# A third LayerNorm row buffer in the output stage, gate/up sums made there, and other moves in a two-layer transformer kernel

## The chip, the cores and the metric

The kernel runs on one core of a Trainium2 chip. The metric is the device time of one execution in microseconds (us).

## The reference

Two layers, each an attention block with a linear kernel (block A) and a gated feed-forward block (block B), on a sequence of 2048 rows of 1024 values, in bfloat16:

```python
def reference(A_x, A_wqkv, A_wo, B_x, B_w_gate, B_w_up, B_w_down):
    def _A_ref(x, wqkv, wo):              # 32 heads of 32
        ...                               # q, k, v = x @ wqkv
        phi = lambda t: jnp.where(t > 0, t + 1, jnp.exp(t)) + 1e-6
        pq, pk = phi(q), phi(k)
        kv = jnp.einsum("bhsd,bhse->bhde", pk, v)
        z = jnp.einsum("bhsd->bhd", pk)
        num = jnp.einsum("bhqd,bhde->bhqe", pq, kv)
        den = jnp.einsum("bhqd,bhd->bhq", pq, z)[..., None] + 1e-6
        ...                               # (num / den) @ wo
    def _B_ref(x, w_gate, w_up, w_down):  # 3584 hidden values
        ...                               # ((x @ w_gate) * (x @ w_up)) @ w_down
    x = A_x
    x = x + _A_ref(_layernorm(x, axis=-1), A_wqkv, A_wo)
    x = x + _B_ref(_layernorm(x, axis=-1), B_w_gate, B_w_up, B_w_down)
    x = x + _A_ref(_layernorm(x, axis=-1), A_wqkv, A_wo)
    x = x + _B_ref(_layernorm(x, axis=-1), B_w_gate, B_w_up, B_w_down)
    return x
```

## The kernel before

In each layer the stages are: projections of q and k in "quads" of pairs, a stage that forms the small key/value products ("G stage"), the last held projections, the output stage (the product with `wo`, row tile by row tile), then gate/up and down in two passes of half the sequence. The gate/up and down products are done by a two-level scheme that replaces some matmuls by sums of blocks (Strassen's idea), and VectorE makes those sums.

Three pieces of it carry the argument. The first is the norm of a row of queries. There are two buffers for the finished row (`asb`), but one for the reciprocals (`rden`):

```python
def norm(i):
    ...                                            # VectorE: product, reduction, add
    P.add("dve", lambda e: e.reciprocal(rden, den), ...)
    b = i % 2
    P.add("pool", lambda e: e.tensor_tensor(out=asb[b]..., in1=rden..., op=ALU.mult), ...)
    P.add("sp", lambda e: e.dma_start_transpose(xnT[:, :, i * 128:(i + 1) * 128], asb[b]), ...)
```

The second is the loop of the output stage. `norm`, `pack` (a copy of weights from DRAM to DRAM), `ring_issue` (weight loads) and `step_t` (the transpose of a LayerNorm row) all put their transfers into one queue, that of SyncE (SP):

```python
for i in range(NST):                               # 16 row tiles
    if na[0] < NST:
        if i % 3 == 2:
            norm(tok[na[0]]); na[0] += 1
    elif RG["n"] < NR:
        ring_issue()
    if first and i % 3 == 1:
        pack()
    nxt.step_t(1)                                  # transpose of a LayerNorm row, by DMA
    nxt.b1_one()
    if i >= 2:
        nxt.start(i - 2)                           # statistics of a row, VectorE
    y_grp(tok[i], 0, i)                            # 8 matmuls, then an add on VectorE
    y_seed(i + 1)                                  # ScalarE seeds a bank for the next row
    nxt.b2_one()                                   # ScalarE normalises a row into O_XN[n % 2]
    y_grp(tok[i], 1, i)                            # 8 matmuls, then a copy on ScalarE
    ...
    if nxt.t_next >= 8 and RG["tq"] is None:       # eight rows transposed:
        RG["tq"] = t_ops(0)                        # block sums of the first half, VectorE
    ...
```

The third is the head of a gate/up pass, where the first layer makes the sums for its first two units just before the first matmuls, and the second layer issues the loads of its block sums:

```python
pre = ("P1A", "P1B") + (("D2A", "D2B") if jit else ()) + ("P5A", "P5B")
...
if jit:                                            # first layer, first pass
    prep_s(n0)                                     # four sums on VectorE
    prep_s(n0 + 1)
early = not first
if early:
    for q in "25":
        sums(1, q)                                 # second layer: loads from scratch
for tk in pre:
    emit(0, tk, True)
```

Of the kernel before, what the change touches and what calls it, by code (L numbers as in the profile page):

```python
# [180 lines left out]
def build_kernel(nc, A_x, A_wqkv, A_wo, B_w_gate, B_w_up, B_w_down, out):  # L181
    _, S, D = A_x.shape
# [55 lines left out]
    O_DEN = take(128)  # L238
    O_RDEN = take(128)
    O_RZ = take(64)  # L240
# [66 lines left out]
    KTA = [dkey("ta%d" % i) for i in range(2)]  # L307
    KTL = [dkey("tl%d" % i) for i in range(2)]
    KTF = [dkey("tf%d" % i) for i in range(NST)]
# [12 lines left out]
    with ExitStack() as es:  # L322
# [48 lines left out]
        den = vf(O_DEN, 32)  # L371
        rden = vf(O_RDEN, 32)
        rz = vf(O_RZ, 8)
# [101 lines left out]
        class LN:  # L475
# [12 lines left out]
            def dst(self, n):  # L488
                if self.to == "A0":
                    return xrt[n], r_xr(n)  # L490
                return xn[n % 2], R(O_XN[n % 2], D * 2)

# [42 lines left out]
            def transpose(self, n):  # L535
                d, r = self.dst(n)
                i = self.order[n]
                if self.use_dma:
                    P.add("sp", lambda e: e.dma_start_transpose(xnT[:, :, i * 128:(i + 1) * 128], d),
                          rd=r, wr=r_xT(i * 128, (i + 1) * 128), dma_sem=KTF[i] if self.to == "A0" else KTL[n % 2])  # L540
                    return
# [320 lines left out]
        def layer_A(lnp, nxt, first):  # L862
# [147 lines left out]
            def norm(i):  # L1010
# [7 lines left out]
                      rd=R(O_DEN, 128), wr=R(O_DEN, 128))  # L1018
                P.add("dve", lambda e: e.reciprocal(rden, den), rd=R(O_DEN, 128), wr=R(O_RDEN, 128))  # L1019
                b = i % 2  # L1020
                P.add("pool", lambda e: e.tensor_tensor(out=asb[b].rearrange("p (h c) -> p h c", c=32), in0=pbuf.rearrange("p (h c) -> p h c", c=32),  # L1021
                                                       in1=rden.unsqueeze(2).broadcast_to([128, 32, 32]), op=ALU.mult),
                      rd=R(O_P[i % 2], D * 4) + R(O_RDEN, 128), wr=R(O_A[b], D * 2))
                P.add("sp", lambda e: e.dma_start_transpose(xnT[:, :, i * 128:(i + 1) * 128], asb[b]),
# [70 lines left out]
            for n, (kind, p) in enumerate(items):  # L1095
# [10 lines left out]
                if first:  # L1106
                    i = NPL + len(LNX) + n
                    for j in range(2):
                        if i < NST:
                            job(n, 2 * j, lambda i=i, j=j: lnstep(i, j))  # L1110
                    c, m = 9 - max(NPL - 3, 0), len(items)
                    if (n + 1) * c // m > n * c // m:
                        job(n, 3, pack)
                elif n >= 2:
                    if n == 9:
                        job(n, 0, lambda: rl.update(o=O_XN[0]))
                    job(n, 0, lnp.flush_b)
                    job(n, 2, lnp.flush_a)

# [136 lines left out]
            for i in range(NST):  # L1256
# [9 lines left out]
                nxt.b1_one()  # L1266
                if i >= 2:
                    nxt.start(i - 2)
                y_grp(tok[i], 0, i)
                y_seed(i + 1)  # L1270
                nxt.b2_one()
                y_grp(tok[i], 1, i)
                if not first and i >= 8:
                    stash(i - 8)
# [8 lines left out]
        def layer_B(lnp, nxt, first):  # L1283
# [6 lines left out]
            if not is_last:  # L1290
                nxt.use_dma = True
                nxt.on_act = False

# [195 lines left out]
            def gateup(ps_, ticks, l2):  # L1489
# [16 lines left out]

                pre = ("P1A", "P1B") + (("D2A", "D2B") if jit else ()) + ("P5A", "P5B")
                tpl = tp_ops(ps_, l2)
# [44 lines left out]

                if jit:
                    prep_s(n0)
                    prep_s(n0 + 1)
                early = not first
                if early:
                    for q in "25":
                        sums(1, q)  # L1560
                for tk in pre:
                    emit(0, tk, True)
                for p in range(NP):
                    for tk in order:
                        emit(p, tk)
# [19 lines left out]
            def down(ps_, ticks, tail):  # L1585
# [37 lines left out]
                tr, ha_ = [flat(O_T + 3584 * i) for i in range(3)], [flat(O_HA + 3584 * i) for i in range(4)]  # L1623
                sbuf2 = {"4": [xbuf(i) for i in range(3)], "5": tr if "4" in l2d else [xbuf(i) for i in range(3)], "3": [xbuf(i, 1 - ps_) for i in range(3)]}
                tbuf2 = {"4": [flat(RE), flat(RE + 3584), flat(O_XN[0])], "5": [xbuf(3), ha_[0], ha_[1]], "3": [ha_[2], ha_[3], xbuf(3, 1 - ps_)]}
                r4 = [(vf(o, 512), R(o, 2048)) for o in (RC, RC + 2048, RB + 28672, RB + 30720)]
# [184 lines left out]
            def dticks0(q, t):  # L1811
# [5 lines left out]
                if q == "3" and t < 2:  # L1817
                    tq.pop(0)()
                    tq.pop(0)()
                if q == "5" and t == 3 and not is_last:  # L1820
                    for k in range(4):
# [8 lines left out]
            def dticks1(q, t):  # L1830
# [11 lines left out]
                if q == "7" and t == 3:  # L1842
                    for c in (2, 4):
                        tw_load("q", c)
                if q == "5" and t == 3:
                    for w in "kq":
# [5 lines left out]
                if q == "3":  # L1852
                    s_make(nxt.order, 0)[t]()
                    stash(12 + t)
# [18 lines left out]
            lnp.use_dma = False  # L1873
            lnp.on_act = False
        dh0 = D // 2
        dma(x_res[:, 0, 0:dh0], x2[0:128, 0:dh0], r_x(0, 0, dh0), KX[0])
# [62 lines left out]
```

## Time and profile before

| | kernel before |
|---|---|
| median time | 1449.56 us (3 runs, 1448.41 to 1450.8) |
| span of the profiled execution | 1449.1 us (run of 1450.86 us) |
| TensorE busy | 1426.2 us, 98% |
| VectorE / ScalarE / GpSimd busy | 84% / 46% / 10% |
| idle time of TensorE in its waits view | 19.4 us |

TensorE is the bound, and the only thing to win is its idle time. The prediction shows where that lies. Two lines more are from the waits views of ScalarE and VectorE of the kernel before; after the colon stand the sum in us, the number of times, and the longest.

```profile
ACT arena L468 <- DMA arena<-arena: 16.3, 7, 4.2
DVE arena L765 <- DMA arena<-arena: 7.1, 2, 4.6
```

L468 is the normalisation of a row on ScalarE, L765 a block sum on VectorE. Both wait for a DMA inside the on-chip memory, that is, for a transpose.

### The profile page before, as it was taken

How to read it: one execution, taken by the hardware profiler on the slowest of the kernel's cores; microseconds unless marked ns; L12 is line 12 of the kernel's file. 1: busy time of each engine (PE TensorE's matmuls, PEld its weight loads, DVE VectorE, ACT ScalarE, POOL GpSimd, SP SyncE). 2: the span in 40 equal slices, each digit the busy share in tenths (PEclk: the TensorE clock that was granted, in tenths of full speed). 3: DMA queues.
4: the chain of work that ended last, by engine and by line, in shares of the span. 5: the costliest groups of instructions: out<-in, count | busy, mean ns of one | idle time of the engine just before them, and what ended most of it. 6: DMA issues, size and time to landing. Idle time of an engine off the chain costs nothing.

```text
span 1449.1 us, 21876 instructions
## 1 busy us (share of the span) xinstructions
PE 1426.2 (98%) x8186; PEld 787.3 (54%) x8186; DVE 1218.2 (84%) x2376; ACT 665.6 (46%) x1378; POOL 147.2 (10%) x176
## 2 busy tenths in 40 slices
PE   8999998999999999999999999999999999999999
PEld 3444443455545666664554444446666475666547
DVE  6987887999978799988779878778888887888888
ACT  5673245444420266661037823467776004777400
POOL 2212521000010000002010046210000100000000
PEclk9999999999999999999999999999999999999999
DMA  8578977997786777777985166667775866777653
GB/s 261 88 203 225 198 171 155 289 328 266 266 252 215 235 248 260 245 256 264 268 262 145 40 175 151 184 166 263 261 260 191 277 237 231 265 259 257 207 195 119
DMA packets 270459, 320.22 MB, mean 221 GB/s; under 512 B 161936, under 2 KB 212880, under 8 KB 270352
## 3 DMA queue, kind: packets, MB, share of 16 engines
q1 hardware_dynamic: 270352, 318.82, 72.3%
q8 instruction: 64, 1.05, 0.3%
q14 instruction: 43, 0.35, 0.1%
HBM read 236.45 MB, written 73.40 MB: 214 GB/s over the span
## 4 chain that ended last, share of the span: by engine, by line
PE 80%; DVE 11%; DMA 4%; issue 2%; ACT 2%; POOL 1%; SPq 1%; POOLq 0%; DVEq 0%; ACTq 0%
PE ps L1319 27%; PE ps L1400 16%; PE ps L1736 14%; PE ps L919 6%; PE ps L1138 6%; PE ps L1654 5%; DVE arena L765 3%; PE ps L890 3%; DMA arena<-arena 3%; PE ps L1240 2%; DVE arena L451 2%; DVE arena L768 1%; DVE arena L1015 1%; DVE arena L1012 1%; DVE arena L612 1%
## 5 line engine op out<-in xcount | busy, mean ns | idle before, releaser
L765 DVE TENSOR_TENSOR arena<-arena 128x512 f16<-128x512 f16 (+8 forms) x1015 | 497.8, 518 | 61.6 <-ACT arena L1404 33.6
L1319 PE MATMUL ps<-arena 128*128 128x512 f16 x1888 | 457.3, 379 | 2.7 <-ACT ps L1348 2.0
L768 DVE SCALAR_TENSOR_TENSOR arena<-ps,arena 128x512 f16<-128x512 f32 (+3 forms) x545 | 353.6, 664 | 68.7 <-PE ps L1736 26.9
L1400 PE MATMUL ps<-arena 128*128 128x256 f16 x2184 | 287.5, 273 | 2.2 <-DMA arena<-sp_scratch 1.3
L1319 PEld LDWEIGHTS ps<-arena 128*128 128x128 f16 (+1 forms) x1888 | 182.8, 98 | 165.6 <-ACT ps L1348 6.3
L1400 PEld LDWEIGHTS ps<-arena 128*128 128x128 f16 (+1 forms) x2184 | 212.1, 98 | 93.1 <-ACT arena L1404 6.9
L1736 PE MATMUL ps<-arena 128*128 128x512 bf16 (+1 forms) x1120 | 244.7, 379 | 0.0
L1736 PEld LDWEIGHTS ps<-arena 128*128 128x128 f16 x1120 | 109.6, 98 | 130.2
L1324 ACT ACTIVATE arena<-ps 128x512 f32<-128x512 f32 x224 | 133.7, 597 | 82.2 <-PE ps L1319 64.3
L1404 ACT ACTIVATE arena<-ps 128x256 f32<-128x256 f32 x351 | 125.1, 385 | 26.9 <-PE ps L1400 22.0
L919 PE MATMUL ps<-arena 128*128 128x512 f16 (+1 forms) x560 | 123.2, 379 | 2.7 <-ACT arena L926 0.9
L1138 PE MATMUL ps<-arena 128*128 128x512 bf16 x512 | 116.1, 379 | 0.0
L1240 PE MATMUL ps<-arena 128*128 128x512 bf16 x512 | 111.5, 379 | 3.6 <-ACT ps L1234 3.3
L454 POOL TENSOR_SCALAR arena<-arena 128x1 f32<-128x1 f32 x64 | 24.5, 383 | 804.5 <-DVE arena L453 804.5
L1410 ACT COPY ps<-ps 128x256 f32<-128x256 f32 x182 | 66.4, 365 | 75.0 <-DVE arena L768 29.4
L451 DVE BATCH_NORM_STATS2 arena<-arena 128x6 f32<-128x512 bf16 x128 | 88.2, 689 | 13.9 <-DMA arena<-in_A_x_dram 6.6
L1021 POOL TENSOR_TENSOR arena<-arena 128x1024 f16<-128x1024 f32 x32 | 76.4, 2389 | 184.3 <-DVE arena L1019 167.1
L1348 ACT COPY ps<-ps 128x512 f32<-128x512 f32 x112 | 65.4, 584 | 61.4 <-PE ps L1319 50.2
L1682 ACT COPY arena<-ps 128x256 f32<-128x256 f32 x8 | 3.0, 372 | 197.1 <-PE ps L1654 197.1
L919 PEld LDWEIGHTS ps<-arena 128*128 128x128 f16 x560 | 54.0, 98 | 70.9 <-ACT arena L926 5.1
L890 PE MATMUL ps<-arena 128*128 128x512 bf16 x384 | 85.5, 379 | 3.6 <-ACT arena L555 1.6
L1654 PE MATMUL ps<-arena 128*128 128x256 f16 (+1 forms) x784 | 86.8, 273 | 0.5 <-DVE arena L768 0.3
(61 smaller groups left out, 969.8 us busy)
## 6 DMA issues: line engine op xcount, KB each, us to landing
arena<-w_scratch SPq DMA_DIRECT2D x84, 896.0 KB, 4.6
arena<-t_scratch SPq DMA_DIRECT2D x32, 896.0 KB, 5.8
arena<-in_B_w_down_dram SPq DMA_DIRECT2D x24, 896.0 KB, 5.0
arena<-sp_scratch SPq DMA_DIRECT2D x26, 768.0 KB, 4.2
w_scratch<-arena SPq DMA_DIRECT2D x28, 512.0 KB, 6.3
arena<-w_scratch SPq DMA_DIRECT2D x28, 384.0 KB, 5.2
x_scratch<-arena SPq DMA_DIRECT2D x40, 256.0 KB, 7.4
arena<-x_scratch SPq DMA_DIRECT2D x40, 256.0 KB, 5.9
```

Of the source, the lines that this page charges most:

```text
L765: P.add("dve", lambda e: e.tensor_tensor(out=out, in0=a, in1=b, op=op), rd=rd, wr=wr, prd=prd)
L768: P.add("dve", lambda e: e.scalar_tensor_tensor(out=out, in0=a, scalar=sc, in1=b, op0=ALU.mult, op1=op1), rd=rd, wr=wr, prd=prd)
L890: return [e.matmul(psb(bank), xnT[:, k, i * 128:(i + 1) * 128], t[:, k, h * 512:(h + 1) * 512], start=(k == 0), stop=(k == KT - 1)) for k ...
L919: P.add("pe", lambda e: [e.matmul(psb(bank), a[0][:, k, :], b[0][:, k, :], start=(q in (1, 5) and k == 0), stop=(k == 3), skip_group_check ...
L1138: return [e.matmul(psb(bank), xrt[t][:, jj * 128:(jj + 1) * 128], pk[:, h, t, :], start=(t == tok[0]), stop=(t == tok[NST - 1])) for t in ts]
L1240: return [e.matmul(psb(bank), xnT[:, g, i * 128:(i + 1) * 128], wp[:, g, dh * 512:(dh + 1) * 512], start=(dh == 0 and g == 0), stop=(g == ...
L1319: P.add("pe", lambda e: [e.matmul(psb(bank), w[:, k, :], x[:, k, :], start=(start and k == 0), stop=(k == 3), skip_group_check=True) for k ...
L1324: P.add("act", lambda e: e.activation(t, psb(bank), AF.Copy, scale=SG), prd=[bank], wr=r)
L1400: P.add("pe", lambda e: [e.matmul(psb(bank)[:, 256 * half:256 * half + 256], w[:, k, :], xx[:, k, :], start=(start and k == 0), stop=(k == ...
L1404: P.add("act", lambda e: e.activation(d, src, AF.Copy, scale=sc), prd=[xk], wr=rd_)
L1654: P.add("pe", lambda e: [e.matmul(psb(bank)[:, 256 * half:256 * half + 256], a[:, k, 128 * r:128 * r + 128], b[:, k, :], start=(start and ...
L1736: P.add("pe", lambda e: [e.matmul(psb(bank), hv[:, 7 * hf + k, t * 128:(t + 1) * 128], w[:, k, :], start=(q in "15" and hf == 0 and k == 0 ...
```

## The change

The intent is to close TensorE's gaps by giving the engines that feed it more room. It has five parts: (1) two reciprocal buffers; (2) a third row buffer for LayerNorm rows in the output stage; (3) the first gate/up sums made in the last two rows of the output stage, with the statistics of one row and a normalisation moved behind the first matmuls of gate/up; (4) in the layer change, statistics started in every second quad only, ScalarE normalising under down, and block sums of the next layer made under the fifth product rather than the third; (5) one block-sum load issued under down. The diff, cut to its core:

```diff
-    O_RDEN = take(128)
+    O_RDEN = [take(128) for _ in range(2)]
...
-                return xn[n % 2], R(O_XN[n % 2], D * 2)
+                o = (O_XN + [O_WQ])[n % 3] if self.to == "B" and n < 14 else O_XN[n % 2]
+                return vh(o, D), R(o, D * 2)
...
-                    job(n, 2, lnp.flush_a)
+                    if n % 2:
+                        job(n, 2, lnp.flush_a)
...
-                if i >= 2:
+                if 2 <= i < 15:
                     nxt.start(i - 2)
                 y_grp(tok[i], 0, i)
                 y_seed(i + 1)
-                nxt.b2_one()
+                if i < 15:
+                    nxt.b2_one()
                 y_grp(tok[i], 1, i)
+                if first and i >= 14:
+                    prep_s(i - 14)
...
-                nxt.on_act = False
+                nxt.on_act = True
...
-                pre = ("P1A", "P1B") + (("D2A", "D2B") if jit else ()) + ("P5A", "P5B")
+                pre = ("P1A", "P1B", "P5A", "P5B")
...
-                if jit:
-                    prep_s(n0)
-                    prep_s(n0 + 1)
                 early = not first
                 if early:
-                    for q in "25":
+                    for q in "25"[ps_:]:
                         sums(1, q)
                 for tk in pre:
                     emit(0, tk, True)
+                if ps_ == 0:
+                    lnp.b2_one()
+                    lnp.start(13)
...
+                if q == "4" and t == 0 and not first:
+                    sp_load(1, 1, "2")
...
+                if q == "5":
+                    s_make(nxt.order, 0)[t]()
...
                 if q == "3":
-                    s_make(nxt.order, 0)[t]()
```

Cut are the new semaphores, the use of `rden[i % 2]`, and a shift of scratch buffers for the moved block sums.

More of the change, by code (lines that the diff above doesn't have):

```diff
@@ L307, in build_kernel @@
     KTA = [dkey("ta%d" % i) for i in range(2)]
-    KTL = [dkey("tl%d" % i) for i in range(2)]
+    KTL = [dkey("tl%d" % i) for i in range(3)]
     KTF = [dkey("tf%d" % i) for i in range(NST)]
@@ L371, in build_kernel @@
         den = vf(O_DEN, 32)
-        rden = vf(O_RDEN, 32)
+        rden = [vf(o, 32) for o in O_RDEN]
         rz = vf(O_RZ, 8)
@@ L539, in transpose @@
                     P.add("sp", lambda e: e.dma_start_transpose(xnT[:, :, i * 128:(i + 1) * 128], d),
-                          rd=r, wr=r_xT(i * 128, (i + 1) * 128), dma_sem=KTF[i] if self.to == "A0" else KTL[n % 2])
+                          rd=r, wr=r_xT(i * 128, (i + 1) * 128), dma_sem=KTF[i] if self.to == "A0" else KTL[n % (3 if self.to == "B" and n < 14 else 2)])
                     return
@@ L1018, in norm @@
                       rd=R(O_DEN, 128), wr=R(O_DEN, 128))
-                P.add("dve", lambda e: e.reciprocal(rden, den), rd=R(O_DEN, 128), wr=R(O_RDEN, 128))
+                P.add("dve", lambda e: e.reciprocal(rden[i % 2], den), rd=R(O_DEN, 128), wr=R(O_RDEN[i % 2], 128))
                 b = i % 2
                 P.add("pool", lambda e: e.tensor_tensor(out=asb[b].rearrange("p (h c) -> p h c", c=32), in0=pbuf.rearrange("p (h c) -> p h c", c=32),
-                                                       in1=rden.unsqueeze(2).broadcast_to([128, 32, 32]), op=ALU.mult),
-                      rd=R(O_P[i % 2], D * 4) + R(O_RDEN, 128), wr=R(O_A[b], D * 2))
+                                                       in1=rden[b].unsqueeze(2).broadcast_to([128, 32, 32]), op=ALU.mult),
+                      rd=R(O_P[i % 2], D * 4) + R(O_RDEN[b], 128), wr=R(O_A[b], D * 2))
                 P.add("sp", lambda e: e.dma_start_transpose(xnT[:, :, i * 128:(i + 1) * 128], asb[b]),
@@ L1623, in down @@
                 tr, ha_ = [flat(O_T + 3584 * i) for i in range(3)], [flat(O_HA + 3584 * i) for i in range(4)]
-                sbuf2 = {"4": [xbuf(i) for i in range(3)], "5": tr if "4" in l2d else [xbuf(i) for i in range(3)], "3": [xbuf(i, 1 - ps_) for i in range(3)]}
-                tbuf2 = {"4": [flat(RE), flat(RE + 3584), flat(O_XN[0])], "5": [xbuf(3), ha_[0], ha_[1]], "3": [ha_[2], ha_[3], xbuf(3, 1 - ps_)]}
+                sbuf2 = {"4": [xbuf(i) for i in range(3)], "5": tr if "4" in l2d else [xbuf(1 + i) for i in range(3)], "3": [xbuf(i, 1 - ps_) for i in range(3)]}
+                tbuf2 = {"4": [flat(RE), flat(RE + 3584), flat(O_XN[0])], "5": [xbuf(3) if "4" in l2d else ha_[2], ha_[0], ha_[1]], "3": [ha_[2], ha_[3], xbuf(3, 1 - ps_)]}
                 r4 = [(vf(o, 512), R(o, 2048)) for o in (RC, RC + 2048, RB + 28672, RB + 30720)]
@@ L1874, in layer_B @@
             lnp.on_act = False
+            if not is_last:
+                nxt.on_act = False
         dh0 = D // 2
```

## The prediction

> **What bounds the kernel now.** I read the page's busy shares first, then the times of the slices, then the waits of TensorE, then its timeline gap by gap.
>
> ```profile
> PE 1426.2 (98%) x8186; PEld 787.3 (54%) x8186; DVE 1218.2 (84%) x2376; ACT 665.6 (46%) x1378; POOL 147.2 (10%) x176
> PEclk9999999999999999999999999999999999999999
> ```
>
> TensorE (PE) is busy 98% of the 1449.1 us and its clock is granted in full, so it is the bound almost everywhere, and nothing in the diff takes a matmul away. What can be won is idle time of TensorE. The waits view of TensorE has 19.4 us of it, and the timeline puts it into 23 places. Those that the change can touch:
>
> ```profile
> 180.49 1.04 PE L1191 MATMUL ps<-arena 128*128 128x512 bf16 x4 [1.07 <-DVE arena L1169]
> 185.06 0.39 PE L1191 MATMUL ps<-arena 128*128 128x512 bf16 x1 [1.15 <-DVE arena L1198]
> 225.26 12.26 PE L1240 MATMUL ps<-arena 128*128 128x512 bf16 x56 [1.69 <-ACT ps L1234]
> 237.75 7.08 PE L1240 MATMUL ps<-arena 128*128 128x512 bf16 x32 [0.23 <-DVE arena L1246]
> 248.54 4.49 PE L1319 MATMUL ps<-arena 128*128 128x512 f16 x20 [1.98 <-ACT ps L1348]
> 253.72 6.22 PE L1319 MATMUL ps<-arena 128*128 128x512 f16 x28 [0.69 <-ACT arena L1324]
> 774.72 1.04 PE L919 MATMUL ps<-arena 128*128 128x512 bf16 x4 [0.73 <-DVE arena L939]
> 776.27 6.33 PE L919 MATMUL ps<-arena 128*128 128x512 f16 x28 [0.51 <-ACT arena L926]
> 938.96 21.33 PE L1240 MATMUL ps<-arena 128*128 128x512 bf16 x98 [1.63 <-ACT ps L1234]
> 1212.72 0.60 PE L1400 MATMUL ps<-arena 128*128 128x256 f16 x4 [1.25 <-DMA arena<-sp_scratch]
> ```
>
> Columns: start, length, engine, line, operation, count, and in brackets the idle time before it with what ended it. Two more of the kind, 0.19 and 0.20 us at 782.80 and 789.21, wait for L926. These twelve places hold 11.3 us. The start of the kernel (five gaps, 5.6 us, until 14.65) is untouched, and so are a few small gaps in the gate/up and down stages (2.5 us).
>
> One correction. In steady state eight 512-column matmuls follow each other in 1.73 us (216 ns each), yet one is drawn 379 ns long. The drawn end overlaps the next start by about 0.16 us, so each gap really costs about 0.17 us more than is printed: 11.3 + 12 x 0.17 = 13.3 us. That is the ceiling of this change, 0.9% of the time.
>
> **What the Trainium skill says.** "TensorE: Matmul & The Clock Gate", section "Back-to-back issue gap", gives N/2.4 + 2.5 ns for a matmul by itself, 216 ns at N = 512, and 131 ns for a long stream; the trace's 1.73 us for eight in a stream agrees with the first, not with the second. Over 8186 matmuls this makes an estimated 1419 us of pure issue: the time can't fall far. "Perfetto Trace Analysis", section "Tensor Engine Instruction (MATMUL, LD_WEIGHTS)", says that ScalarE (ACT), VectorE (DVE) and GpSimd (POOL) run their instructions strictly in order; the ACT lines below agree, where one waiting instruction holds up two that TensorE needs. The same page, section "Optimization Strategy", connects gaps with too few buffers and advises making what ends them start sooner, which is the plan of the change. "SBUF — State Buffer", section "SBUF: two separate sides", says that VectorE and GpSimd take a shared port pair as an exclusive lock: VectorE's L1017 takes 181 ns alone and up to 1342 ns beside GpSimd's L1021, so the trace fits. This makes me cautious about the first part below.
>
> **The change part by part.**
>
> *1. Two `rden` buffers.* Before 180.49 the chain is: GpSimd's L1021 waits for a DMA, VectorE's reciprocal L1019 waits for L1021 because there is one `rden`, and L1169, which TensorE needs, stands behind it.
>
> ```profile
> DVE arena L1019 <- POOL arena L1021: 2.8, 1, 2.8
> ```
>
> This wait occurs once. With two buffers L1169 can run when its matmuls end, near 177.9, before TensorE asks for it at 179.3. The two gaps are 2.22 + 0.34 = 2.56 us. But VectorE's next small instruction L612 took 1.68 us beside L1021 instead of 0.28 and may do so again, and then L1198 still comes late for the second gap. I count 1.5 us.
>
> *2. Third row buffer for the LayerNorm rows in the output stage.* ScalarE normalises a row (L468, 1.24 us), a DMA transposes it, and with two buffers row n waits for the transpose of row n-2.
>
> ```profile
> 222.88 1.24 ACT L468 ACTIVATE arena<-arena 128x1024 f16<-128x1024 bf16 x1 [2.99 <-DMA arena<-arena]
> 224.02 0.56 ACT L1248 CAST arena<-ps 128x512 bf16<-128x512 f32 x1
> 224.62 0.59 ACT L1234 CAST ps<-arena 128x512 f32<-128x512 bf16 x1
> ```
>
> The copy L1234 seeds a bank for TensorE and stands behind L468; the 1.69 us gap at 225.26 ends with it. The transpose's median from issue to landing is 3.5 us after about 1.3 us of issue, one row of the loop is 16 matmuls or 3.46 us: with two buffers that is just not enough, with three the row has one loop step more. All L468 waits for DMA sum to 16.3 us in seven places, and most should go. VectorE gains too: its first block sum of the stage waits 4.59 us (until 234.21) for the eighth transpose, which then lets it fall behind at 237.75. Worth: 1.86 + 0.40 in the first layer, 1.80 in the second: 4.1 us, of which I count 4.0. No work is added; the three buffers lie in space that is free then.
>
> *3. First gate/up sums in the output stage, last LayerNorm row after the first matmuls.* At 248.54 TensorE waits for the copies L1348, which stand on ScalarE behind L468 and L1248, themselves behind a late VectorE. VectorE's statistics and final add end at 248.39, then it makes eight sums (3.01 us). After the change these eight are issued in the last two rows, statistics of row 13 (two of 0.69, one of 0.21) and one L468 move behind the first sixteen matmuls, and the D2 products, which need the copies, no longer come ahead of P5. The two gaps are 2.67 + 0.34 = 3.0 us. VectorE's load in the last five rows is then about 3.75 + 3.75 + 4.97 + 4.0 + 2.35 = 18.8 us (from 0.2, 1.6, 0.65, 1.22 and 1.5 us for the five kinds of work in a row) against 17.3 us of TensorE. It ends about 1.5 us late, just in time for P5, but the statistics follow, and the first pair was already tight (VectorE 12.3 of 13 us busy from 249 to 262). I count 2.3 us.
>
> *4. Spread LayerNorms, normalising on ScalarE under down, block sums of pair 0 earlier.* In the second attention layer four statistics come in four successive quads before and in every other quad after. From 753 to 789 VectorE is busy 34.8 of 36 us, and the four gaps there are 1.63 + 0.68 = 2.3 us. Each statistics costs 1.6 us, each normalisation 0.53 us (L471), and about two of the four move out of the full stretch, so the backlog of 1 to 2 us should go. One normalisation that ScalarE inherits lands in a quad where it is already busy about 4.9 of 6 us. Under down ScalarE is nearly free (3.7 of 79 us), and TensorE has no gap there, so moving about ten L471 there (some 5 us of VectorE) gains nothing by itself. I count 1.6 us.
>
> *5. Block sums loaded under down.* The first two-level product of the last gate/up pass waits 1.25 us for its load; issued more than 10 us earlier, it has landed. 1.4 us, counted in full.
>
> Sum: 1.5 + 4.0 + 2.3 + 1.6 + 1.4 = 10.8 us. I take off 1.8 us for new gaps, of which I expect some: statistics inside the first pair, relu buffers that share the LayerNorm row buffer from the tenth quad on, now soon after a later transpose. Predicted: 1449.6 - 9.0 = 1440.6, say 1440.5 us.
>
> **The rivals.** *VectorE takes over as the bound at the seam.* Its work isn't less, only moved; from 235 to 249 it is busy 13.3 of 14 us. Then TensorE meets it a few microseconds later in the first pair, and parts 2 and 3 give 3 us rather than 6.3: 1444. For it speaks the tight first pair; against it the 4.6 us idle before 234.21 and 2.57 us before 224.69, which part 2 frees. *The transposes are held up by the in-order DMA queue, not by buffers.* Around 201 to 210 an L468 row's transpose was issued behind one of L1021's that waited for GpSimd until 209. Then a third buffer only moves the wait: part 2 gives 1 us, total 1443.5. Against it: later in the stage no such transpose is in the way, and the waits go on. *New waits outweigh*: the relu buffer's wait for the transpose costs 2 to 4 us in one quad, ScalarE stalls on L468 while copies queue behind it under down: 1446. *Everything goes and the seams run clean*: 13.3 us, 1436.
>
> **Range and chances.** The ceiling gives 1436, the worst believable mixture of rivals about 1446.5; between them the centre is 1440.5. Low 1436.5, high 1446.5. Faster by over 2% needs 29 us, more than twice all the gaps that are touched: 0.01. Slower by over 2% needs a new wait that repeats in each pair, for which I see no cause: 0.01. Within 2%: 0.98.
>
> **What would show it.** TensorE's idle near 1426 us of busy time falls from 19.4 to about 10 us. Right if: no L1019 wait for L1021; L468 waits for DMA under 5 us; no gap over 0.5 us on L1234 in either output stage; the gaps on L1348 and on sp_scratch gone; L926 and L939 gaps under 0.7 us in sum. Wrong if: gaps on VectorE's L765 or L768 appear in the first gate/up pair, ScalarE waits for a transpose before a relu in the quads, or L1198's gap at 185 stays, which would show the port lock and not `rden` as its cause. Everything falls if the same gaps stand under other names.

## The result, and the profile after

The changed kernel takes **1441.08 us** (median of 4 runs, 1439.98 to 1441.79), the kernel before 1449.26 us (4 runs, 1448.41 to 1450.8). The ratio is 0.9942, with a 95% interval of 0.9924 to 0.9959: the same within 2%, and some 8 us faster. (Here and below, a ratio is the mean time of one kernel's fast runs over that of the other's of the same rounds, so it isn't quite the ratio of the medians.) The prediction was 1440.5 us, so number and class were right. The reasons were only partly right, as will be seen. TensorE's idle time in its waits view fell from 19.4 to 10.2 us; about 10 was forecast.

The page of the changed kernel, busy time of each engine:

```profile
PE 1421.8 (99%) x8126; PEld 787.8 (55%) x8186; DVE 1213.8 (84%) x2376; ACT 680.2 (47%) x1389; POOL 148.9 (10%) x176
```

60 matmul records are missing here (8126, not 8186), and so the busy time of TensorE is too small and can't be compared with before. This trace shows the start of some stages one matmul (0.22 us) off, so differences of 0.2 us between stages are not read.

TensorE's timeline at the seam between output stage and gate/up of layer 1 (start, length, engine, line, operation, count, idle time before and what ended it), and the answers to the two waits above. L468 kept its number; L765 and L768 are now L766 and L769, L1240 (output matmuls) is L1242, L1319 (gate/up matmuls) is L1324:

```profile
233.22 7.08 PE L1242 MATMUL ps<-arena 128*128 128x512 bf16 x31 [0.18 <-DVE arena L1248]
243.65 5.35 PE L1324 MATMUL ps<-arena 128*128 128x512 f16 x24 [0.76 <-DVE arena L766]
249.96 4.49 PE L1324 MATMUL ps<-arena 128*128 128x512 f16 x20 [0.96 <-DVE arena L769]
```

```profile
ACT arena L468 <- DMA arena<-arena: 13.0, 6, 3.9
```

```profile
DVE arena L766 <- DMA arena<-arena: 6.3, 2, 4.5
```

The gaps of 1.69 us behind the seed are gone, and those of 1.98 and 0.69 us in gate/up are replaced by 0.76 and 0.96 us, now behind VectorE's block sums. ScalarE's waits for transposes didn't vanish. The view sums over the whole kernel; on ScalarE's timeline, all 16.3 us of the kernel before lie in the two output stages (11.0 in the first layer), and of the 13.0 us after the change 9.1 lie there (5.3 in the first layer). The other 3.9 us are one wait at 680.8 us, under down, where ScalarE normalises only since the change.

For the rest I took from the timelines of TensorE the time of the first matmul of each stage. The next table has the length of each stage that moved, in us. Both kernels were profiled a second time in the experiments; the last column is an experiment described below. Of the changed kernel, only the second profile has all 8186 records.

| stage | before, 1st profile | before, 2nd | changed, 1st | changed, 2nd | changed, transpose first |
|---|---|---|---|---|---|
| held projections, layer 1 | 11.43 | 8.89 | 8.86 | 8.86 | 8.86 |
| output, layer 1 | 57.66 | 57.42 | 55.61 | 55.58 | 55.25 |
| gate/up, layer 1, first pass | 166.37 | 166.37 | 165.47 | 165.25 | 163.40 |
| quads, layer 2 | 91.36 | 91.37 | 89.96 | 89.97 | 89.95 |
| output, layer 2 | 57.06 | 57.09 | 55.25 | 55.25 | 55.25 |
| gate/up, layer 2, second pass | 157.51 | 157.90 | 156.31 | 156.09 | 156.31 |
| down, layer 2, second pass | 88.10 | 88.12 | 87.53 | 87.83 | 87.54 |
| whole span | 1449.14 | 1446.51 | 1438.27 | 1438.48 | 1436.19 |

All other stages agree within 0.5 us, except for the first projections, 74.4 to 75.3 us in any kernel.

### The profile page after: what moved, and what is told of

Its sections match the earlier page's. It is cut to its first block, busy times and chain, and to the rows that moved or that the text cites. A ratio compares the mean times of both kernels' runs of the same rounds, so it can differ in the third digit from the quotient of the medians.

```text
span 1438.3 us, 21791 instructions
## 1 busy us (share of the span) xinstructions
PE 1421.8 (99%) x8126; PEld 787.8 (55%) x8186; DVE 1213.8 (84%) x2376; ACT 680.2 (47%) x1389; POOL 148.9 (10%) x176
## 4 chain that ended last, share of the span: by engine, by line
PE 87%; DVE 7%; DMA 2%; issue 2%; ACT 1%; POOL 0%; SPq 0%; DVEq 0%; ACTq 0%
PE ps L1324 28%; PE ps L1741 17%; PE ps L1405 17%; PE ps L1140 8%; PE ps L920 6%; PE ps L1659 5%; PE ps L1242 4%; PE ps L891 3%; DVE arena L766 2%; DVE arena L451 1%; DMA arena<-arena 1%; DVE arena L769 1%; DVE arena L613 1%; DMA arena<-in_A_wqkv_dram 1%; PE ps L1166 0%
## 5 line engine op out<-in xcount | busy, mean ns | idle before, releaser
L766 DVE TENSOR_TENSOR arena<-arena 128x512 f16<-128x512 f16 (+8 forms) x1015 | 497.8, 518 | 59.8 <-ACT arena L1409 34.1
L1324 PE MATMUL ps<-arena 128*128 128x512 f16 x1888 | 457.2, 379 | 1.8 <-DVE arena L769 1.0
L769 DVE SCALAR_TENSOR_TENSOR arena<-ps,arena 128x512 f16<-128x512 f32 (+3 forms) x545 | 353.9, 664 | 69.4 <-PE ps L1741 28.4
L1324 PEld LDWEIGHTS ps<-arena 128*128 128x128 f16 (+1 forms) x1888 | 182.9, 98 | 164.4 <-ACT ps L1353 3.8
L1140 PE MATMUL ps<-arena 128*128 128x512 bf16 x498 | 114.7, 379 | 0.7
L1242 PE MATMUL ps<-arena 128*128 128x512 bf16 x502 | 110.5, 379 | 0.7 <-DVE arena L1248 0.2
L1022 POOL TENSOR_TENSOR arena<-arena 128x1024 f16<-128x1024 f32 x32 | 77.2, 2414 | 156.4 <-DVE arena L1020 142.0
L891 PE MATMUL ps<-arena 128*128 128x512 bf16 x375 | 84.6, 379 | 4.2 <-ACT arena L556 1.6
L1418 DVE TENSOR_TENSOR ps<-ps,arena 128x256 f32<-128x256 f32 x182 | 76.7, 428 | 10.5 <-PE ps L1405 9.5
```

Source lines behind the costliest of these rows:

```text
L766: P.add("dve", lambda e: e.tensor_tensor(out=out, in0=a, in1=b, op=op), rd=rd, wr=wr, prd=prd)
L769: P.add("dve", lambda e: e.scalar_tensor_tensor(out=out, in0=a, scalar=sc, in1=b, op0=ALU.mult, op1=op1), rd=rd, wr=wr, prd=prd)
L891: return [e.matmul(psb(bank), xnT[:, k, i * 128:(i + 1) * 128], t[:, k, h * 512:(h + 1) * 512], start=(k == 0), stop=(k == KT - 1)) for k ...
L1140: return [e.matmul(psb(bank), xrt[t][:, jj * 128:(jj + 1) * 128], pk[:, h, t, :], start=(t == tok[0]), stop=(t == tok[NST - 1])) for t in ts]
L1242: return [e.matmul(psb(bank), xnT[:, g, i * 128:(i + 1) * 128], wp[:, g, dh * 512:(dh + 1) * 512], start=(dh == 0 and g == 0), stop=(g == ...
L1324: P.add("pe", lambda e: [e.matmul(psb(bank), w[:, k, :], x[:, k, :], start=(start and k == 0), stop=(k == 3), skip_group_check=True) for k ...
```

## The experiments

Theory: the prediction's five parts, each with its size. Rivals: the one in-order queue, not the number of buffers, holds the rows up; the moved sums only shift a wait; a gap in one profile is chance. Twelve kernels ran, each correct. Nearly all have the reading of their stages as the verdict, as 1 us is less than the times alone resolve.

### Controls: both kernels again

> The kernel before, unchanged, run and profiled once more, since one reciprocal buffer in the changed kernel did not bring back the 2.6 us of the held-projection stage. Theory A (the 2.6 us belong to the kernel before): the stage takes 11.4 us again, GpSimd's second-last multiplication waits 3 us or more for a transpose to land. Theory B (they were chance in one profile, a transpose that landed late): the stage takes about 8.9 us in this profile, span some 2.5 us shorter than the 1449.1 of the first profile.

> The changed kernel, unchanged, as a control beside the others of this call. Expected: 1441 us (1440 to 1442), each stage within 0.3 us of its first profile, apart from the first 20 us, whose loads vary; output stages 55.6 and 55.3, first gate/up stage 165.5. If the held-projection stage is above 10 us here, its length is chance and not the change's.

**Kernel before:** 1450.18 us (5 runs, 1447.41 to 1451.49; ratio to the other 9 runs of the same kernel 0.9992, interval 0.998 to 1.0005). **Changed kernel:** 1440.59 us (5 runs, 1440.19 to 1440.79), ratio 0.993 (0.9916 to 0.9944).

The held projections took 8.89 us in this second profile of the kernel before, not 11.43. Theory B holds for these 2.6 us. The first profile of before had, on GpSimd's and VectorE's timelines:

```profile
177.52 1.91 POOL L1021 TENSOR_TENSOR arena<-arena 128x1024 f16<-128x1024 f32 x1 [3.76 <-DMA arena<-arena]
179.54 0.35 DVE L1019 RECIPROCAL arena<-arena 128x32 f32<-128x32 f32 x1 [2.77 <-POOL arena L1021]
179.81 0.63 DVE L1169 TENSOR_TENSOR arena<-ps,arena 128x512 bf16<-128x512 f32 x1
```

The second profile of the same kernel has this:

```profile
174.26 1.92 POOL L1021 TENSOR_TENSOR arena<-arena 128x1024 f16<-128x1024 f32 x1 [1.66 <-DVE arena L1012]
176.27 0.35 DVE L1019 RECIPROCAL arena<-arena 128x32 f32<-128x32 f32 x1
177.59 0.69 DVE L1169 TENSOR_TENSOR arena<-ps,arena 128x512 bf16<-128x512 f32 x1 [0.96 <-PE ps L1164]
```

GpSimd's multiplication started at 174.26 and not at 177.52, with VectorE as the last thing that it waited for and not a transpose. L1169 was then held only by its own matmuls. The span was 1446.5 us rather than 1449.1, and most of that difference is this one stage.

### One reciprocal buffer, and two alone

In the changed kernel:

```diff
-  e.reciprocal(rden[i % 2], den)      # and likewise in GpSimd's multiplication
+  e.reciprocal(rden[0], den)
```

> The changed kernel with one reciprocal buffer again, all else kept. Theory: the whole 2.6 us that the held-projection stage lost came from the second buffer, so that stage goes back from 8.9 to about 11.4 us in the profile, VectorE's reciprocal again waits for GpSimd's multiplication, no other stage moves by more than 0.4 us, and the time rises by about 2.5 us (1441 to 1443.6). Rival: the stage became shorter through something else in the change (other order of VectorE and GpSimd work, the clash on their shared port); then it stays under 10 us and the time rises by less than 1.2 us.

Measured: the held projections took 8.92 us. The theory, as written, fell: undoing the part brought nothing back in that stage. The time was 1442.26 us (1441.83 to 1442.39), 1.7 us above the control of the other call; in the profile (1.4 us above) the extra sat in the first projections (75.14 us, against 74.47 in the control) and in the first down pass of layer 2 (0.55 us in its main part and 0.40 in its two-level part). In the first of these the granted clock was 0.82 from 5 to 10 us and 0.84 from 10 to 15, where the control has 1.0; in the second TensorE waited 0.59 us for VectorE's L766. I know of no path from the reciprocals to these stages, so why they came in this execution stays open.

> The kernel before with the second reciprocal buffer and nothing else. Theory A (the single buffer makes VectorE wait for GpSimd and holds up TensorE): the held-projection stage falls from 11.4 to about 8.9 us and the time by 2.5 us against the kernel before of the same call. Theory B (chance in a transpose's landing): the stage differs from that of the other profile of the kernel before by whatever chance gives, 8.9 in both if that one has 8.9, and the medians differ by less than 1 us. In both, VectorE's reciprocal no longer waits for GpSimd.

Measured: 8.96 us in the stage, against 8.89 with one buffer. The median was 1448.64 us (1447.64 to 1449.63), the ratio 0.9985 (0.9972 to 0.9997), while the kernel before against itself gave 0.9992 (0.998 to 1.0005). The intervals overlap. The stage reads as theory B; the medians are 1.5 to 2 us apart, which hints at a gain in other executions without showing it; the clock differs too (three of the five runs of the kernel before were at 0.998 or less, one of these five).

### The late transpose, forced

If chance decides whether the transpose is late, the mechanism must be tested with a transpose that is always late. One more pack of weights goes into the queue ahead of it:

```diff
                 if first and n % 2 == 0:
                     pack()
+                    if n == 12:
+                        pack()
```

> The kernel before with one weight pack more, two copies of 256 KB, pushed into the queue just ahead of the transpose for which GpSimd's second-last multiplication of the norm waits (one pack fewer later). It makes that transpose late on purpose, with one reciprocal buffer. Theory (late transpose, then GpSimd, then the reciprocal behind it in VectorE's order, then TensorE): the held-projection stage takes 11.4 us or more. Rival (the first profile's stall had another cause): 8.9 to 9.3 us.

> The same late transpose, forced in the same way, with two reciprocal buffers. Theory (the second buffer lets VectorE go on while GpSimd waits): the held-projection stage stays at 8.9 to 9.4 us, at least 2 us below the same stage with one buffer. Rival (the second buffer is of no use, since VectorE is then held by the next thing GpSimd owes it): as long as with one buffer, within 0.5 us.

Measured with one buffer: 1454.52 us (4 runs, 1452.19 to 1455.78), stage 11.34 us. With two: 1449.18 us (4 runs, 1448.09 to 1451.38), stage 10.06 us. GpSimd and VectorE with one buffer:

```profile
178.30 1.91 POOL L1021 TENSOR_TENSOR arena<-arena 128x1024 f16<-128x1024 f32 x1 [4.61 <-DMA arena<-arena]
180.32 0.35 DVE L1019 RECIPROCAL arena<-arena 128x32 f32<-128x32 f32 x1 [3.62 <-POOL arena L1021]
181.27 1.04 PE L1191 MATMUL ps<-arena 128*128 128x512 bf16 x4 [0.98 <-DVE arena L1169]
```

The same with two (lines of VectorE, GpSimd and TensorE):

```profile
176.30 0.35 DVE L1019 RECIPROCAL arena<-arena 128x32 f32<-128x32 f32 x1
...
178.27 3.83 POOL L1021 TENSOR_TENSOR arena<-arena 128x1024 f16<-128x1024 f32 x2 [4.98 <-DMA arena<-arena]
...
180.98 1.28 DVE L612 TENSOR_SCALAR arena<-arena 128x512 bf16<-128x512 bf16 x1
...
184.36 0.39 PE L1191 MATMUL ps<-arena 128*128 128x512 bf16 x1 [1.03 <-DVE arena L1198]
```

The chain of the prediction is shown: a late transpose, GpSimd behind it, the reciprocal behind GpSimd, TensorE behind the copy. With two buffers the reciprocal goes at 176.30 and the first gap is gone. The second gap stays at 1.03 us: VectorE's L612 takes 1.28 us beside GpSimd's two multiplications, and 0.28 us where GpSimd is idle. So the second buffer takes away 1.28 us in these two profiles, half of the stall, and neither theory's number is right: less than the 2 us of the first, more than the rival's nothing. The medians differ by more, 5.3 us. The profiled run of the one-buffer kernel was the fastest of its four and that of the other the slowest, so what the other executions lost isn't seen in a profile.

One candidate is the clock. In the profile with two buffers, right behind TensorE's gap at the seam, the granted clock was 0.62 from 248 to 250 us and 0.52 from 250 to 252, and then 1.0 again. The 20 matmuls there, which take 4.49 us in the kernel before, took 6.18:

```profile
247.90 6.18 PE L1321 MATMUL ps<-arena 128*128 128x512 f16 x20 [1.99 <-ACT ps L1350]
```

So this execution lost 1.7 us there, and its first gate/up pass took 168.28 us (166.68 with one buffer). The three executions with one buffer that weren't profiled had mean clocks of 0.996 to 0.998, the four with two buffers 0.999 to 1.0. As an estimate, 0.002 of 1450 us is 3 us, so the clock may account for more of the 5.3 us than the buffer does. What lowers it, and whether longer gaps do, no run here tests.

### Two row buffers

```diff
-  o = (O_XN + [O_WQ])[n % 3] if self.to == "B" and n < 14 else O_XN[n % 2]
+  o = O_XN[n % 2]                     # and two semaphores
```

> The changed kernel with two LayerNorm row buffers again, all else kept. Theory: both output stages grow back, the first from 55.6 to about 57.7 us, the second from 55.3 to about 57.1, ScalarE's normalizations wait for a transpose 7 times for some 16 us again in layer 1, and the time rises by about 3.9 us (1441 to 1445). First rival: the third buffer was idle, because the transposes land in the order of one queue anyway, and the two stages became shorter by the other parts (the two rows and sums moved over the seam); then both stages stay within 0.5 us of 55.5 and the time within 1 us. Second rival: what the two stages lose comes back in the stages behind them, as their gaps at the seam are waits for the same late transpose; then the time rises by less than 2 us.

Measured: 1444.15 us (1443.38 to 1444.31), 3.4 us above the kernel of the next experiment, which is as fast as the changed one (1440.71); the output stages grew to 57.21 and 57.03 us. TensorE's timeline has the two gaps again:

```profile
222.47 19.28 PE L1242 MATMUL ps<-arena 128*128 128x512 bf16 x86 [1.68 <-ACT ps L1236]
...
933.30 22.62 PE L1242 MATMUL ps<-arena 128*128 128x512 bf16 x102 [1.60 <-ACT ps L1236]
```

The theory holds; 3.4 us are nearly all of the expected 3.9, and nothing comes back in later stages (first gate/up pass 165.46 us). ScalarE's waits for transposes are back as well: 18.5 us in seven, in both output stages together.

### Sums back at the seam

```diff
-                if first and i >= 14:
-                    prep_s(i - 14)
...
+                if jit:
+                    prep_s(n0)
+                    prep_s(n0 + 1)
```

and the two D2 products back ahead of P5, as before.

> The changed kernel with the first gate/up block sums made at the start of the gate/up stage again, all else kept (the last two LayerNorm rows stay where the change put them). Theory: the move gained the 0.9 us that the first gate/up stage lost, so that stage goes from 165.5 to about 166.4 us and the time rises by 1 to 2 us; VectorE has the same work, only later, so its lateness at the seam grows. Rival: the move only shifted the wait, since VectorE runs without a pause from the landing of the eighth transpose to after the seam in either case; then the new gaps of 0.76 and 0.96 us go, the old ones come back, and the time stays within 0.5 us.

Measured: 1440.71 us (1440.33 to 1441.93), no different from the changed kernel. The first gate/up stage took 166.02 us (165.25 in the control), the output stage 55.41 (55.58). TensorE's gaps at the seam:

```profile
248.50 2.76 PE L1322 MATMUL ps<-arena 128*128 128x512 f16 x12 [0.69 <-ACT arena L1327]
252.23 3.63 PE L1322 MATMUL ps<-arena 128*128 128x512 f16 x16 [0.97 <-DVE arena L769]
```

The gap at VectorE's L766 (0.76 us) is exchanged for one of 0.69 us at a copy of ScalarE, and the one at L769 stays. The rival holds in the time, with a remainder of 0.6 us: the move shifted a wait. The old gap of 1.98 us did not come back, so its going is not due to the moved sums or products.

### The row's transpose ahead of the norm's block

One line of the changed kernel's loop is moved:

```diff
             for i in range(NST):
+                nxt.step_t(1)
                 if na[0] < NST:
                     if i % 3 == 2:
                         norm(tok[na[0]])
...
-                nxt.step_t(1)
                 nxt.b1_one()
```

> The changed kernel with one line moved: in the output stage's loop the LayerNorm row's transpose is issued ahead of the norm's block, not behind it, so that it does not stand in the one in-order queue behind a transpose that waits for GpSimd. Theory (order of the queue holds up the eighth row): ScalarE's waits for a transpose in the stage fall from 13.0 us to under 8, VectorE's wait of 4.5 us for the eighth transpose falls under 2.5 us, the gaps of 0.76 and 0.96 us at the seam shrink by half or more, and the time falls by 0.8 to 1.7 us (1441 to about 1440). Rival (it is the time from issue to landing, and the weight packs in the same queue): the waits change by less than 1 us each and the time by less than 0.4 us.

Measured: **1437.86 us** (4 runs, 1437.75 to 1438.42), ratio to before 0.9917 (0.9904 to 0.9931). This is the fastest kernel; its runs all lie below the lowest of the changed kernel's, 1439.98. They were run at other times. The queue of SP in the changed kernel (L1025 is the transpose of a norm's row, L540 that of a LayerNorm row; a line's length is the issue alone):

```profile
198.31 3.29 SPq L540 DMA_TRANSPOSE arena<-arena  x1
...
206.60 1.24 SPq L1025 DMA_TRANSPOSE arena<-arena  x1
207.89 1.33 SPq L540 DMA_TRANSPOSE arena<-arena  x1
```

The row that is sent at 207.89 was ready at 200.92 (L468 began at 199.68 and takes 1.24 us). It stood 7.0 us behind the norm's block, which sends two transfers (the code above leaves out the first): a load of a row of x, which went at 202.75, and the transpose, which waited until 206.58 for GpSimd (L1022 began at 204.66 and took 1.92 us). SP issued nothing from 203.11 to 206.60. After the move:

```profile
202.49 2.09 SPq L540 DMA_TRANSPOSE arena<-arena  x1
...
206.97 1.24 SPq L1025 DMA_TRANSPOSE arena<-arena  x1
```

Here the same row was ready at 201.30 and went at 202.49. The waits of ScalarE (over the whole kernel; the one that is left lies under down, at 678.8 us, so that the output stages have none) and of VectorE, and TensorE at the seam:

```profile
ACT arena L468 <- DMA arena<-arena: 4.0, 1, 4.0
```

```profile
DVE arena L766 <- DMA arena<-arena: 1.9, 2, 1.2
```

```profile
240.16 12.25 PE L1324 MATMUL ps<-arena 128*128 128x512 f16 x56
```

No idle time is printed before it, and its 56 matmuls follow each other: both gaps at the seam are gone. The first gate/up pass took 163.40 us, 1.85 us below the control (2.07 below the first profile). The time fell by 2.8 us against the kernel of the previous experiment, where 0.8 to 1.7 was expected. The theory holds, with a larger effect. Whether it is the norm's block or the weight loads and packs ahead of the row that cost most isn't told apart, as the one line moves past all of them.

### The same line in the kernel before, and with two row buffers

> The kernel before, with two row buffers and one reciprocal buffer, and only the row's transpose issued ahead of the norm's block in the output stage's loop. Theory A (the order of the one queue is what holds the rows up, the third buffer only hides it): both output stages fall to 55.3 to 55.8 us (57.4 and 57.1 before), and the time falls by 3.5 us or more (1450 to 1446.5). Theory B (two buffers are too few in any order): the first output stage falls by less than 0.7 us, the second, where fewer rows stand behind a norm, by less than 0.3, and the time falls by about 1 us or less. Beside this it is one more profile of the held-projection stage with a single reciprocal buffer: 8.9 or 11.4 us, as chance has it.

Measured: 1446.94 us (1446.08 to 1447.56), ratio 0.9975 (0.9962 to 0.9987), 4.1 us below the 9 runs of before (1451.05). The output stages took 55.95 and 55.25 us. Theory A holds but for 0.15 us in the first stage: with the right order, two buffers suffice to close TensorE's gaps behind the seed. ScalarE still waits 9.8 us for transposes in the output stages, about as long as with three buffers in the old order (9.1); only order and third buffer together take these waits away. The held projections took 10.20 us here, again another value with one reciprocal buffer.

The next kernel is the changed one with the line moved, two row buffers, and part of the layer change undone:

```diff
+                nxt.step_t(1)               # ahead of the norm's block
...
+  o = O_XN[n % 2]                           # two row buffers
...
-                nxt.on_act = True
+                nxt.on_act = False          # VectorE normalises under down
...
-                if q == "5":
-                    s_make(nxt.order, 0)[t]()
                 if q == "3":
+                    s_make(nxt.order, 0)[t]()
```

> The changed kernel with the transpose issued ahead of the norm's block, but with two row buffers, and, in other stages, the block sums of the layer change back under the third product and their normalizations back on VectorE. Theory A on the buffers (the right order makes the third one needless): output stages 55.3 to 55.8 and 55.3 us. Theory B (two are too few in any order): 56.5 us or more in at least one, TensorE's gaps of 1.7 us behind the seed on ScalarE stay. Theory on the sums (starting the statistics in every second quad is what shortened the quads of layer 2, and the moved sums gave nothing): quads of layer 2 at 90.0 within 0.3 us; rival: the moved sums and ScalarE carry part of it, quads at 90.5 or more. No time is predicted from it beyond 1437.9 plus what these stages lose.

Measured: 1441.53 us (1440.54 to 1441.76). The output stages took 55.97 and 55.25 us, but the first gate/up pass 165.48, with its gaps of 0.8 and 1.0 us at L766 and L769 back. So theory A holds, nearly, for the output stages alone (0.7 us more than the 55.25 with three buffers): at the seam it takes both the right order and the third buffer. VectorE waited 4.9 us for the eighth transpose here and in the kernel before with the line moved, against 1.2 with both. The quads of layer 2 took 89.63 us, 0.3 less than in the changed kernel. The sums moved to the fifth product and the normalisation on ScalarE gained nothing there.

### Statistics in every quad, and the block-sum load issued early

```diff
-                    if n % 2:
-                        job(n, 2, lnp.flush_a)
+                    job(n, 2, lnp.flush_a)
...
-                    for q in "25"[ps_:]:
+                    for q in "25":          # and no load under down
```

> The changed kernel with two parts undone that lie in different stages: the LayerNorm statistics of the layer change are started in every quad again and not in every second, and the block-sum load of the second pass of layer 2 is issued early again. Theory: the quads of layer 2 go from 89.96 back to 91.4 us, the last gate/up stage from 156.3 to 157.5, no other stage moves by over 0.3, and the time rises by 2.6 us (1441 to 1443.7). Rival for the first: what shortened the quads was the block sums moved under the fifth product and the normalizations put on ScalarE; then the quads stay within 0.4 us of 90. Rival for the second: the load is in time either way and TensorE's wait is for VectorE; then the last gate/up stage stays at 156.3.

Measured: 1443.79 us (1442.65 to 1445.16), 3.2 us above the control. The quads of layer 2 took 91.80 us (89.97 in the control), the last gate/up pass 157.53 (156.09). Two of the gaps in the quads and the one in gate/up:

```profile
768.79 1.04 PE L920 MATMUL ps<-arena 128*128 128x512 bf16 x4 [0.83 <-DVE arena L940]
770.34 6.32 PE L920 MATMUL ps<-arena 128*128 128x512 f16 x28 [0.51 <-ACT arena L927]
...
1204.67 0.60 PE L1404 MATMUL ps<-arena 128*128 128x256 f16 x4 [1.28 <-DMA arena<-sp_scratch]
```

Both theories hold. The one line about the statistics gives 1.8 us, more than all of part 4, and the load gives 1.4.

## Why the prediction was right or wrong

The number was right because the large terms were right and the allowance for new gaps covered the parts that were counted too high. That is partly luck: part 1 was worth nothing in the second profiles and part 3 gave less than half of what was counted, while the allowance of 1.8 us, which made up for this, was meant for the quads too, where no gap came. The expected gain was 9.0 us; the medians give 8.2 us in the first call and 9.6 in the control's, and the second profiles 8.0. Runs at a mean clock of 1.0 alone, 1448.8 us (ten of the kernel before) and 1440.8 us (five of the changed kernel), lie 8 us apart, so some of the 9.6 goes with the clock. Point by point:

**The bound.** Right: what was won is idle time of TensorE, and its matmuls stayed as they were. In the fastest kernel the 256 matmuls of the output stage take 55.25 us, 216 ns each. The correction for the drawn end was right too: in the output stage of layer 2 one gap of 1.63 us went, and the stage became 1.81 us shorter in profiles with all records (57.06 to 55.25), 0.18 more than printed.

**Part 1, counted at 1.5 us.** The mechanism is shown, and the caution about L612 was right: with a late transpose the second buffer is worth 1.28 us in the stage, and L1198's gap stays. The step that failed is that it "occurs once" was read as once in every execution. In four profiles of kernels with one buffer and no forced delay the stage took 11.43, 8.89, 8.92 and 10.20 us, so a mean of 9.9, or 1.0 us above the 8.9 without any wait. What the part is worth is some 0 to 1.3 us in the profiles, by chance. The forced pair's medians, and the kernel before with this part alone, hint at more; but their clocks differ too, so that isn't shown.

**Part 2, counted at 4.0 us.** The size was nearly right: 3.4 us by undoing it. A step was wrong: L468's waits were to fall under 5 us, and in the output stages fell from 16.3 to 9.1 (10.4 in the second profile); VectorE's wait for the eighth transpose stayed at 4.5 us. A third buffer gave TensorE's seeds enough room, but left the rows in front of the same queue. The prediction took the waits to be the buffers' alone. The runs show two causes: the third buffer alone leaves 9.1 us, the order alone 9.8 (7.6 beside the other parts), and both together none. So the rival that I had put at "part 2 gives 1 us", the in-order queue, was right about half of the cause and wrong about the price. My argument against it, that no such transpose is in the way later in the stage, doesn't hold with three buffers: the waits of 1.11, 1.69 and 2.52 us at 211 to 220 us of the changed kernel, after that transpose, are gone when only the order is changed, so a row that was late once kept the next ones late. With two buffers such waits do go on in the right order (1.11, 1.18 and 2.76 us). "Perfetto Trace Analysis", section "DMA Instruction — HWDGE (DVE, Sync)", puts the semaphore wait of a DMA into the sequencer, ahead of its issue, and the data movement outside the profiled window; the case agrees, with the 3.5 us in which SP issued nothing before the waiting transpose though the next one was ready, and with issues of 1.24 us beside 3.1 to 5.8 us from issue to landing for the LayerNorm rows of this stage.

**Part 3, counted at 2.3 us.** Mis-sized: the stage gained 0.9 to 1.1 us, of which moving the sums is 0.6, with nothing of it measurable in the time. The step that failed is that VectorE would end "just in time for P5": it can only begin its block sums after the eighth transpose, at 229.68, and it still sat idle for 4.54 us before that, so its work reached the seam late wherever it stood in the program. The first rival, VectorE taking over at the seam, came true in its form (gaps at L766 and L769, one of the prediction's own signs of being wrong), but in part: parts 2 and 3 gave 4.8 us by the stages, between the 6.3 counted and the rival's 3. The missing 2 us are what the moved line recovers.

**Part 4, counted at 1.6 us.** Right in size (1.40). The statistics carry all of it; the rest of the part gave nothing in the quads, as the prediction said of the work under down.

**Part 5, counted at 1.4 us.** Right: 1.2 in the first pair of profiles, 1.4 by undoing it.

**New gaps, 1.8 us.** Expected in the first pair and in the quads. They came in the first pair (0.76 and 0.96 us); the quads had none.

## What to carry to other kernels

Before adding a buffer, look at the queue that fills it: a transfer which is ready but stands behind one that still waits can cost as much as a missing buffer, and moving one line in the issue order may be worth as much as more memory; here each alone left 7.6 to 10.4 of some 16 us of ScalarE's waits, and only both removed them. A gap that one profile shows once may belong to that execution only, so take a second profile of the unchanged kernel before counting on it, and read each run's mean clock before explaining a difference of a few us. When two waits stand in series, as the transpose and VectorE's sums do here, work moved ahead of the second gains little until the first comes earlier.

## What the Trainium skill lacked or had wrong

- "TensorE: Matmul & The Clock Gate", section "Back-to-back issue gap": it gives 131 ns per matmul of 512 columns in a long stream. The runs show 216 ns (256 matmuls in 55.25 us without a gap), the page's figure for a single one.
- "Perfetto Trace Analysis", section "DMA Instruction — HWDGE (DVE, Sync)": it describes one DMA, and leaves to the reader what follows from its table, that a ready DMA waits behind an earlier one that isn't. The runs show a ready row that stood for 7.0 us, and about 3 us of the whole time gained by changing the order.
- No page that I read says how far transposes vary from execution to execution. In one and the same kernel, GpSimd's wait for one transpose put its next row at 177.52 us in one execution and at 174.26 in another, where no transpose held it.
- "SBUF — State Buffer", section "SBUF: two separate sides", agrees in kind with the trace, but gives no figure for such a pair of instructions: a VectorE instruction of 0.28 us (L612) took 1.28 us beside GpSimd. That the lock is the reason wasn't tested by itself.
